# Decay attention with two feed-forward networks: warm-up products ahead of the first flip, the third block's loads between units 11 and 12, plain stores instead of an accumulating one, masks one place sooner

## The chip, the cores and the metric

The kernel runs on one core of a Trainium2 chip. Its engines are TensorE (PE), VectorE (DVE), ScalarE (ACT), GpSimd (POOL) and SyncE (SP), which only issues DMAs here; POOL can issue DMAs too. The metric is the device time of one execution in microseconds, the median of several runs. The granted clock is the share of TensorE's 2.4 GHz that it was given.

## The reference

```python
B, H, S, D = 4, 8, 768, 48                       # attention with a decaying state
for t in range(S):
    cur = einsum('bhd,bhe->bhde', u * k[t], v[t])
    y[t] = einsum('bhd,bhde->bhe', r[t], state + cur)
    state = w[:, :, None] * state + einsum('bhd,bhe->bhde', k[t], v[t])
x = y as (3072 tokens, 384)
x = (silu(x @ w_gate) * (x @ w_val)) @ w_out      # first network, 384 -> 1536 -> 384
h = x @ w_in                                      # second network, 384 -> 2048 -> 384
y = (h * tanh(softplus(h))) @ w_out2
```

## The kernel before

The 768 steps of the sequence are cut into six blocks j of 128; with the four batches b, a block is 512 columns. Each of the two networks multiplies in three products (L247 to L249): the operands are split into a high and a low part of a narrower type, and high by high, high by low and low by high are summed. A **unit** is one block j and one tile f of 128 hidden features of the first network: a gate (nine products into a buffer `mm`), a val (nine more) and, for the unit before, an out (nine into `acc` or `at`). ACT makes the sigmoid of the gate (L659, into a buffer `o`), DVE multiplies (L663), ACT makes the high part (L665, `g_hi`) and DVE the low part (L671, `g_lo`). There are two buffers `mm`, two each of `g_hi` and `g_lo`, and three of `o`.

Work beside the products is put between them by hand. Everything is issued in the order of the program; each engine runs its own instructions in that order, and no other.

- **The early loop** computes the attention of blocks 0 and 1, eight steps (j, b): masks (L479), own terms (L531), outputs (L498), `at_y` (L538), flips (transposes L592) and decays (L415) of the step after next. `warm(n)` puts n products of 128x512 on an idle buffer. Behind the loop the first two loads of block 2 (`rkv_sb`, `n_sb`) are issued.
- **The units** 0 to 13 alternate between block 0 and block 1 for f from 0 to 6; units 14 to 18 finish block 0, units 19 to 23 block 1, and then each block from 2 on has twelve units. The sum of block 1's first seven tiles stands in the `at` buffers (`besides`), is stored to `mid[1]` after unit 13, and the rest is added to it in DRAM by an accumulating DMA of POOL (L698) after unit 23.
- **A tick** decodes one tile of weights, which arrive as 64-bit numbers: ACT L156 and L199, DVE L164, L170, L205 (the tile before), L178 and L183, five DVE operations in a row; the second network's tiles have L205 on POOL and are stored and loaded again. `due` says how many ticks a unit has.
- **The strings `UNITS`** give the order within a unit: `rest` is the low part of the unit before, `mine` that of the unit itself, `fill` a place for steps of the attention of a later block, `tick` a place for a tick. `form` chooses the string. `KEYS`, `STATES`, `AHEAD`, `BEGIN`, `STEPS` and `SPREAD` list the steps that go into the places. In them `first` and `second` are L440 and L442 (POOL), `total` L448 (DVE), `sooner` and `later` L415 (POOL from block 2 on), `diag` two L453 (POOL), `keys` L462, `even` and `odd` the masks (L479) of the two halves of the heads.

The second network reads `mid[j]` back (`load_mid`, L853, three tiles `rows`), and `split_mid` (L861, L862 on DVE) splits them three units later.

Of the kernel before, what the change touches and what calls it, by code (L numbers as in the profile page):

```python
# [9 lines left out]
F32 = mybir.dt.float32  # L10
# [7 lines left out]
P = 128  # L18
CH = 128
NJ = S // CH  # L20
NB = B * CH
# [29 lines left out]
]  # L51
SPREAD = [
    "out state load2 diag1", "hi fade keys1", "low", "sum first2", "scores1 second2",
    "even1 total2", "odd1 later2 sooner2",
]

KEYS = [[(1, b, "keys")] for b in range(B)]
# [11 lines left out]
    "gate act val tick mul tick",  # L69
    "gate rest val act tick out mul tick",  # L70
    "gate tick rest val act fill tick out mul",
    "gate rest fill act val mul tick out fill tick fill tick",
    "gate rest fill act val fill mul mine tick tick out fill",
    "gate fill act val fill mul mine out fill",
    "gate fill act val mul tick mine fill out fill tick tick",
]

# [9 lines left out]
def tile_decay_attention_then_two_ffns(  # L87
# [28 lines left out]

    w2s = [dram.tile([P, 2, DM], F32, name=f"w2s{n}") for n in range(2 * NF2)]
    mid = [dram.tile([P, KC * NB], F32, name=f"mid{j}") for j in range(NJ)]
    ctx.enter_context(tc.manual_schedule())

    class Weights:
# [221 lines left out]
                start=True, stop=True,  # L343
            )

    warm(11)

    scores = [spool.tile([P, NPAIR, CH], F32, name=f"s{g}") for g in range(2)]
    for t in scores:
# [294 lines left out]
                at_part(j, b, part)  # L644


    gs, begun = {}, set()

    def ffn1_mm(j, f, which):
        hi, lo = xs[j, "x"]  # L650
# [23 lines left out]
    def ffn1_out(j, f, first, last):  # L674
        acc = accs
        if (j, f) in BESIDE:

            acc = besides
        if first:
            for m in range(KC):  # L680
                if acc is besides:
                    acc[m] = ps_at.tile([P, NB], F32, name="at")
                else:
                    acc[m] = ps_acc.tile([P, NB], F32, name=f"acc{m}")
        hi, lo = gs.pop((j, f))
        wt = weights.until((1, f, 2))
        for m in range(KC):
            product(acc[m], wt, cols(m), hi, lo, first, last)
        if last:
            for m in range(KC):  # L690
                o = opool.tile([P, NB], F32, name="o")
                if m == 1:
                    nc.vector.tensor_copy(o, acc[m])
                else:
                    nc.scalar.activation(o, acc[m], AF.Copy)
                rows = mid[j][:, m * NB : (m + 1) * NB]
                if j in begun:
                    nc.gpsimd.dma_start(out=rows, in_=o, accum_op=ALU.add)  # L698
                else:
                    nc.sync.dma_start(out=rows, in_=o)  # L700
            begun.add(j)

    class Filler:

# [37 lines left out]
    for n, now in enumerate(early):  # L742
# [14 lines left out]
        at_fade(*now)  # L757
        if now[0] == 0:
            at_state(*now)
        if n + 1 < len(early):  # L760
            at_flip(*now)
        if n >= B - 1:
            weights.tick()

        warm((2, 2, 2, 2, 3, 6, 6, 0)[n])

    for b in range(2):
        at_tiles(EARLY, b)
        load_at(EARLY, b)

# [12 lines left out]
    def unit1(n, fill=nothing, tick=nothing):  # L785

        j, f, _, _ = units[n]
        gate = val = act = None
        form = n if n < 2 else 2 if n < 2 * PAIRED else 3 if n < ready - 1 else 4 if n < ready else 5
        for part in UNITS[form if n < 24 else 6].split():  # L790
            if part == "gate":
                gate = ffn1_mm(j, f, 0)
# [30 lines left out]
    for n in range(len(units) - NF1):  # L823
        if n in beside:
            fill.flush()
            fill = Filler(*beside[n])
        due += 2 if n < 2 * PAIRED else 1.5 if n < ready else 0 if n < 24 else 1.3
        some = int(due) if weights.at < W_STORED + 2 else 0
        ticks = [weights.tick if i < some else nothing for i in range(3)]
        due -= int(due)  # L830
        turn = iter(ticks)
        unit1(n, fill, lambda: next(turn)())
# [16 lines left out]
    def load_mid(j):  # L849
        raw = []  # L850
        for c in range(KC):
            raw.append(mpool.tile([P, NB], F32, name="rows"))
            nc.sync.dma_start(out=raw[c], in_=mid[j][:, c * NB : (c + 1) * NB])  # L853
        xs[j, "m"] = (
            raw,
            *(xpools[j % 2].tile([P, KC, NB], F32R, name=f"x_{k}") for k in ("hi", "lo")),
# [211 lines left out]
```

## Time and profile before

| what | value |
|---|---|
| median of three runs | 970.05 us (968.21 to 971.46) |
| the profiled execution | 971.8 us |
| its span, first to last instruction | 969.8 us |
| PE busy | 949.0 us, 98% of the span |
| DVE, ACT, POOL busy | 635.5, 473.7 and 180.1 us |
| mean granted clock | 0.986 |

PE is the engine to look at: it is busy nearly all the time, so what counts is when it waited and at which clock it ran. In the timeline a row gives start and duration in us, the engine, the line, the operation with its operands and tiles, and in brackets how long the engine was idle ahead of it and which operation ended that idle time.

### The profile page before, as it was taken

What the parts mean: (1) busy time and instruction counts of PE and PEld (TensorE: products, weight loads), DVE (VectorE), ACT (ScalarE), POOL (GpSimd) and SP (SyncE); (2) the same over time, 40 slices, a digit from 0 to 9 for tenths busy, and PEclk for the clock granted to TensorE, in tenths of its full rate; (3) what the DMA queues carried; (4) which work ended last, traced back from release to release, by engine and by line L of the source; (5) the groups of instructions that cost most, each with busy time, mean ns of one, the idle gap of its engine ahead of it and who ended that gap; (6) DMA issues with size and microseconds to landing.
All of it is one profiled execution on the core that took longest, in us unless ns stands there. A gap on an engine that the chain in (4) does not pass through costs nothing.

```text
span 969.8 us, 14841 instructions
## 1 busy us (share of the span) xinstructions
PE 949.0 (98%) x5787; PEld 772.9 (80%) x5787; DVE 635.5 (66%) x1154; ACT 473.7 (49%) x841; POOL 180.1 (19%) x164
## 2 busy tenths in 40 slices
PE   8989998999799999999999999999999999999998
PEld 5868886778688878888888888888888888888886
DVE  7899878634567676832222338878778677787674
ACT  2345543323333433322122238777767676767674
POOL 4220003267565465523000000000000000000000
PEclk8899999999999999999999999999999999999999
DMA  8254433235665675321018640102001010000000
GB/s 324 105 195 147 131 98 109 74 113 152 187 207 190 195 223 185 116 98 50 1 38 270 194 149 1 33 1 66 0 33 33 1 42 25 0 33 1 33 1 32
DMA packets 35781, 94.21 MB, mean 97 GB/s; under 512 B 4224, under 2 KB 4352, under 8 KB 35712
## 3 DMA queue, kind: packets, MB, share of 16 engines
q1 hardware_dynamic: 35280, 92.49, 29.0%
q0 software_dynamic: 432, 0.79, 0.6%
q8 instruction: 45, 0.74, 0.3%
q14 instruction: 24, 0.20, 0.1%
HBM read 70.46 MB, written 22.81 MB: 96 GB/s over the span
## 4 chain that ended last, share of the span: by engine, by line
PE 72%; ACT 1%; DVE 1%; issue 0%
PE acc L247 10%; PE acc L248 10%; PE acc L249 10%; PE mm L247 9%; PE mm L248 9%; PE mm L249 9%; PE at L249 4%; PE at L248 4%; PE at L247 4%; PE at L521 2%; PE at L472 1%; PE at L552 0%; ACT e L908 0%; DVE g_lo L671 0%; DVE s L479 0%
## 5 line engine op out<-in xcount | busy, mean ns | idle before, releaser
L247 PE MATMUL mm<-x_hi,w_split 128*128 128x512 f32 x546 | 217.5, 398 | 5.9 <-DVE o L663 3.7
L248 PE MATMUL mm<-x_lo,w_split 128*128 128x512 f32 x546 | 214.3, 392 | 0.0
L249 PE MATMUL mm<-x_hi,w_split 128*128 128x512 f32 x546 | 213.7, 391 | 0.0
L248 PE MATMUL acc<-g_lo,w_split 128*128 128x512 f32 x483 | 188.7, 391 | 3.8 <-DVE g_lo L671 3.7
L247 PE MATMUL acc<-g_hi,w_split 128*128 128x512 f32 x483 | 189.6, 392 | 0.0
L249 PE MATMUL acc<-g_hi,w_split 128*128 128x512 f32 x483 | 188.3, 390 | 0.0
L663 DVE TENSOR_TENSOR o<-mm,o 128x512 f32<-128x512 f32 x72 | 49.8, 691 | 179.4 <-PE mm L249 143.1
L247 PEld LDWEIGHTS mm<-x_hi,w_split 128*128 128x128 f32 x546 | 103.3, 189 | 30.1 <-DVE o L663 4.2
L249 PEld LDWEIGHTS mm<-x_hi,w_split 128*128 128x128 f32 x546 | 103.4, 189 | 22.1
L248 PEld LDWEIGHTS mm<-x_lo,w_split 128*128 128x128 f32 x546 | 103.5, 190 | 20.7
L665 ACT ACTIVATE g_hi<-o 128x512 fp32r<-128x512 f32 x72 | 45.5, 632 | 137.4 <-DVE o L663 137.1
L248 PEld LDWEIGHTS acc<-g_lo,w_split 128*128 128x128 f32 x483 | 90.8, 188 | 23.5 <-DVE g_lo L671 4.5
L247 PEld LDWEIGHTS acc<-g_hi,w_split 128*128 128x128 f32 x483 | 90.6, 188 | 19.9 <-ACT g_hi L665 0.2
L249 PEld LDWEIGHTS acc<-g_hi,w_split 128*128 128x128 f32 x483 | 90.8, 188 | 18.9
L659 ACT ACTIVATE o<-mm 128x512 f32<-128x512 f32 x72 | 42.8, 594 | 111.0 <-PE mm L249 94.6
L895 ACT ACTIVATE e<-h 128x512 f32<-128x512 f32 x96 | 60.1, 626 | 53.0 <-DVE h L889 51.7
L902 ACT ACTIVATE e<-e 128x512 f32<-128x512 f32 x96 | 59.6, 621 | 49.7 <-DVE e L899 49.6
L909 DVE TENSOR_TENSOR h<-h,e 128x512 f32<-128x512 f32 x96 | 60.0, 688 | 20.5 <-ACT e L908 20.5
L671 DVE TENSOR_TENSOR g_lo<-o,g_hi 128x512 fp32r<-128x512 f32 x72 | 56.1, 780 | 22.4 <-ACT g_hi L665 22.3
L247 PE MATMUL at<-x_hi,w_split 128*128 128x512 f32 x174 | 67.7, 389 | 0.0
L248 PE MATMUL at<-x_lo,w_split 128*128 128x512 f32 x174 | 67.7, 389 | 0.0
L249 PE MATMUL at<-x_hi,w_split 128*128 128x512 f32 x174 | 67.7, 389 | 0.0
(105 smaller groups left out, 1349.5 us busy)
## 6 DMA issues: line engine op xcount, KB each, us to landing
w_raw<-w SPq DMA_DIRECT2D x68, 384.0 KB, 3.4
rkv_sb<-rkv_t SPq DMA_DIRECT2D x16, 768.0 KB, 4.9
w2s<-w_raw SPq DMA_DIRECT2D x32, 384.0 KB, 5.3
w_split<-w2s SPq DMA_DIRECT2D x32, 384.0 KB, 3.6
n_sb<-rk_n SPq DMA_DIRECT2D x16, 384.0 KB, 5.9
mid<-o SPq DMA_DIRECT2D x18, 256.0 KB, 2.3
rows<-mid SPq DMA_DIRECT2D x18, 256.0 KB, 2.6
y<-o SPq DMA_DIRECT2D x18, 256.0 KB, 2.3
```

The costliest lines, as they stand in the source:

```text
L247: nc.tensor.matmul(acc, lhsT=wt[:, 0, sl], rhs=hi, start=start, stop=False)
L248: nc.tensor.matmul(acc, lhsT=wt[:, 0, sl], rhs=lo, start=False, stop=False)
L249: nc.tensor.matmul(acc, lhsT=wt[:, 1, sl], rhs=hi, start=False, stop=stop)
L472: nc.tensor.matmul(ps[g][:, i, :], lhsT=a["k"][q, i, :], rhs=a["r"][q, i, :], start=True, stop=True,)
L521: nc.tensor.matmul(ps[q * QUAD : (q + 1) * QUAD, c, :], lhsT=lhsT, rhs=rhs, start=q not in begun_q, stop=ends[q] == n, skip_group_check=True,)
L659: nc.scalar.activation(sg, ps, AF.Silu)
L663: nc.vector.tensor_tensor(out=sg, in0=ps, in1=sg, op=ALU.mult)
L665: nc.scalar.activation(hi, sg, AF.Copy)
L671: eng.tensor_tensor(out=lo, in0=sg, in1=f32(hi), op=ALU.subtract)
L895: nc.scalar.activation(es[n], hs[n], AF.Exp)
L902: nc.scalar.activation(e, e, AF.Ln, bias=1.0)
L909: nc.vector.tensor_tensor(out=hs[n], in0=hs[n], in1=es[n], op=ALU.mult)
```

## The change

- `warm(11)` at the start becomes `warm(12)`, and in the first step of the early loop four more products stand ahead of the flip.
- The first two loads of block 2 leave their place behind the early loop. They are issued ahead of units 11 and 12.
- The strings of units 14 to 23 change: unit 14 makes the low part of unit 13 and its own, units 15 and on their own low part, ahead of the `out` of the unit before. `due` falls from 1.5 to 1 a unit in units 14 to 18.
- The accumulating DMA goes. Block 1's first sum is stored to a new DRAM tensor `begun`, its second to `mid[1]`, both by SP; `load_mid(1)` loads `mid[1]`, and POOL adds `begun` onto the loaded tiles with an accumulating DMA.
- In `SPREAD` both masks stand where `even` stood, and `total` one place later.

```diff
@@ SPREAD
-    "even1 total2", "odd1 later2 sooner2",
+    "mask1", "total2 later2 sooner2",
@@ UNITS
-    "gate rest fill act val mul tick out fill tick fill tick",
-    "gate rest fill act val fill mul mine tick tick out fill",
-    "gate fill act val fill mul mine out fill",
+    "gate rest fill act val mul tick mine out fill tick fill tick",
+    "gate fill act val mul tick mine out fill tick fill tick",
+    "gate fill act val fill mul mine tick tick out fill",
@@
+    begun = dram.tile([P, KC * NB], F32, name="begun")
@@
-    warm(11)
+    warm(12)
@@ ffn1_out
-                rows = mid[j][:, m * NB : (m + 1) * NB]
-                if j in begun:
-                    nc.gpsimd.dma_start(out=rows, in_=o, accum_op=ALU.add)
-                else:
-                    nc.sync.dma_start(out=rows, in_=o)
-            begun.add(j)
+                to = begun if acc is besides else mid[j]
+                nc.sync.dma_start(out=to[:, m * NB : (m + 1) * NB], in_=o)
@@ the early loop
+        if n == 0:
+            warm(4)
         if n + 1 < len(early):
             at_flip(*now)
@@
-    for b in range(2):
-        at_tiles(EARLY, b)
-        load_at(EARLY, b)
@@ unit1
-        form = n if n < 2 else 2 if n < 2 * PAIRED else 3 if n < ready - 1 else 4 if n < ready else 5
+        form = n if n < 2 else 2 if n < 2 * PAIRED else 3 if n == 2 * PAIRED else 4 if n < ready - 1 else 5
@@ the loop over units
+        if n in (2 * PAIRED - 3, 2 * PAIRED - 2):
+            ahead = order[EARLY * B + n - 2 * PAIRED + 3]
+            at_tiles(*ahead)
+            load_at(*ahead)
-        due += 2 if n < 2 * PAIRED else 1.5 if n < ready else 0 if n < 24 else 1.3
+        due += 2 if n < 2 * PAIRED else 1 if n < ready else 0 if n < 24 else 1.3
@@ load_mid
+            rows = slice(c * NB, (c + 1) * NB)
+            nc.sync.dma_start(out=raw[c], in_=mid[j][:, rows])
+            if j == 1:
+                nc.gpsimd.dma_start(out=raw[c], in_=begun[:, rows], accum_op=ALU.add)
```

Lines below the new ones carry numbers higher by one or two in the changed kernel. On SP, from the last load ahead of the early loop (`u_sb`) on, the rows before are these; `rkv_sb` and `n_sb` are block 2's loads, `w_raw` those of weights, `mid` the stores of the first network:

```order
L325 DMA u_sb<-u_n 128x384
L145 DMA w_raw<-w 128x768 x2
L303 DMA rkv_sb<-rkv_t 128x1536
L304 DMA n_sb<-rk_n 128x768
L303 DMA rkv_sb<-rkv_t 128x1536
L304 DMA n_sb<-rk_n 128x768
L145 DMA w_raw<-w 128x768 x28
L700 DMA mid_114<-o 128x512 x3
```

and now:

```order
L326 DMA u_sb<-u_n 128x384
L146 DMA w_raw<-w 128x768 x24
L304 DMA rkv_sb<-rkv_t 128x1536
L305 DMA n_sb<-rk_n 128x768
L146 DMA w_raw<-w 128x768 x2
L304 DMA rkv_sb<-rkv_t 128x1536
L305 DMA n_sb<-rk_n 128x768
L146 DMA w_raw<-w 128x768 x4
L698 DMA begun<-o 128x512 x3
```

The two pairs of loads moved behind 22 more loads of weights, each pair by itself. On DVE, from the end of unit 15's first tick to the multiply of unit 16, the rows before are (five `w_` rows are a tick, `state` is a sum of the attention's state):

```order
L183 SCALAR_TENSOR_TENSOR w_num<-w_raw,w_num 128x384
L568 TENSOR_TENSOR state<-at,state 48x4x48 x2
L164 TENSOR_SCALAR w_num<-w_num 128x384
L170 SCALAR_TENSOR_TENSOR w_num<-w_raw,w_num 128x384
L205 TENSOR_TENSOR w_split<-w_num,w_split 128x384
L178 TENSOR_SCALAR w_num<-w_num 128x384
L183 SCALAR_TENSOR_TENSOR w_num<-w_raw,w_num 128x384
L671 TENSOR_TENSOR g_lo<-o,g_hi 128x512
L568 TENSOR_TENSOR state<-at,state 48x4x48 x2
L663 TENSOR_TENSOR o<-mm,o 128x512
```

and now, from the multiply of unit 15 on, which the same first tick follows:

```order
L664 TENSOR_TENSOR o<-mm,o 128x512
L165 TENSOR_SCALAR w_num<-w_num 128x384
L171 SCALAR_TENSOR_TENSOR w_num<-w_raw,w_num 128x384
L206 TENSOR_TENSOR w_split<-w_num,w_split 128x384
L179 TENSOR_SCALAR w_num<-w_num 128x384
L184 SCALAR_TENSOR_TENSOR w_num<-w_raw,w_num 128x384
L672 TENSOR_TENSOR g_lo<-o,g_hi 128x512
L569 TENSOR_TENSOR state<-at,state 48x4x48 x4
L664 TENSOR_TENSOR o<-mm,o 128x512
```

The low part (`g_lo`) of unit 15 moved ahead of the sums, and the second tick is gone from between. On POOL, around the accumulating DMA after unit 23, the rows before are:

```order
L453 TENSOR_TENSOR s_230<-ident,bonus 128x512
L205 TENSOR_TENSOR w_raw<-w_num,w_raw 128x384
L462 TENSOR_TENSOR n_sb<-n_sb,tabn 128x384
L698 DMA mid_114<-o 128x512 x3
L440 TENSOR_TENSOR pr<-n_sb 128x384
```

and now:

```order
L454 TENSOR_TENSOR s_232<-ident,bonus 128x512
L206 TENSOR_TENSOR w_raw<-w_num,w_raw 128x384
L463 TENSOR_TENSOR n_sb<-n_sb,tabn 128x384
L441 TENSOR_TENSOR pr<-n_sb 128x384
```

The DMA is gone from there; POOL's last row of all is now the addition in `load_mid`.

## Rows read from the trace of the kernel before

**Rows 1.** Timeline of PE, the rows with the longest waits (in brackets).
```profile
14.63 0.55 PE L592 MATMUL at<-ident,y 128*128 128x128 f32 x3 [1.39 <-DVE y L538]
...
63.11 0.80 PE L247 MATMUL mm<-x_hi,w_split 128*128 128x512 f32 x1 [3.74 <-DVE o L663]
...
164.08 0.50 PE L248 MATMUL acc<-g_lo,w_split 128*128 128x512 f32 x1 [3.67 <-DVE g_lo L671]
...
246.45 0.50 PE L247 MATMUL mm<-x_hi,w_split 128*128 128x512 f32 x1 [2.21 <-ACT o L659]
...
258.43 0.65 PE L521 MATMUL at<-s,rkv_sb 128*32 128x128 f32 x16 [2.69 <-DVE s L479]
```

**Rows 2.** Stretches: length, busy time (instructions) by engine, granted clock, DMA share, GB/s.
```profile
15.00:31.00 16.00, 16.00 (x190) 12.80 (x190) 10.51 (x19) 2.77 (x7) 5.01 (x5) 0.51 0.94 359
160.00:180.00 20.00, 16.32 (x101) 12.29 (x100) 15.84 (x37) 7.24 (x14) 1.06 (x2) 0.91 0.21 60
240.00:260.00 20.00, 15.10 (x130) 11.43 (x129) 11.16 (x19) 6.16 (x14) 13.66 (x12) 0.91 0.62 156
```

**Rows 3.** Timeline of PE, the ninth product after the second wait.
```profile
66.55 0.40 PE L249 MATMUL mm<-x_hi,w_split 128*128 128x512 f32 x1
```

**Rows 4.** Timeline of DVE, one unit with two ticks, undisturbed.
```profile
128.25 0.69 DVE L663 TENSOR_TENSOR o<-mm,o 128x512 f32<-128x512 f32 x1 [0.94 <-PE mm L249]
...
130.80 0.69 DVE L671 TENSOR_TENSOR g_lo<-o,g_hi 128x512 fp32r<-128x512 f32 x1
...
134.37 0.69 DVE L663 TENSOR_TENSOR o<-mm,o 128x512 f32<-128x512 f32 x1 [0.94 <-PE mm L249]
```

**Rows 5.** Timeline of PE, outputs of three steps of the early loop.
```profile
15.85 1.95 PE L498 MATMUL at<-w_split,s 128*64 128x48 f32 x32
...
35.80 1.09 PE L498 MATMUL at<-w_split,s 128*64 128x48 f32 x32
...
40.17 1.19 PE L498 MATMUL at<-w_split,s 128*64 128x48 f32 x32
```

**Rows 6.** SP's timeline, then the page's DMA issues (KB each, us to landing).
```profile
10.97 0.33 SPq L301 DMA_DIRECT2D w_split<-kv_n  x1
...
w_split<-kv_n SPq DMA_DIRECT2D x8, 384.0 KB, 6.7
```

**Rows 7.** Timelines of DVE and (last row) POOL, around unit 0.
```profile
56.65 0.35 DVE L164 TENSOR_SCALAR w_num<-w_num 128x384 f32<-128x384 f32 x1
...
62.38 0.68 DVE L663 TENSOR_TENSOR o<-mm,o 128x512 f32<-128x512 f32 x1
...
71.94 0.69 DVE L671 TENSOR_TENSOR g_lo<-o,g_hi 128x512 fp32r<-128x512 f32 x1
...
59.13 2.91 POOL L415 TENSOR_TENSOR rkv_sb<-rkv_sb,tab 128x512 f32<-128x512 f32 x2
```

**Rows 8.** Timelines of POOL (first row) and DVE, units 15 and 16.
```profile
151.99 2.04 POOL L453 TENSOR_TENSOR s<-ident,bonus 128x512 f32<-128x512 f32 x2 [89.95 <-DVE bonus L448]
...
153.44 0.69 DVE L663 TENSOR_TENSOR o<-mm,o 128x512 f32<-128x512 f32 x1 [1.59 <-PE mm L249]
...
160.65 0.71 DVE L568 TENSOR_TENSOR state<-at,state 48x192 f32<-48x192 f32 x2
...
163.34 0.69 DVE L671 TENSOR_TENSOR g_lo<-o,g_hi 128x512 fp32r<-128x512 f32 x1
```

**Rows 9.** Timeline of ACT around unit 25, then the page's DMA issues.
```profile
245.80 0.60 ACT L659 ACTIVATE o<-mm 128x512 f32<-128x512 f32 x1 [5.77 <-DMA mid<-o]
...
mid<-o SPq DMA_DIRECT2D x18, 256.0 KB, 2.3
...
mid<-o POOLq DMA_DIRECT2D x3, 256.0 KB, 7.0
```

**Rows 10.** Timelines of SP and DVE, block 1's rows in the second network.
```profile
574.97 1.39 SPq L853 DMA_DIRECT2D rows<-mid  x3
...
605.02 0.42 DVE L861 CAST x_hi<-rows 128x512 fp32r<-128x512 f32 x1
```

More of the change, by code (lines that the diff above doesn't have):

```diff
@@ L644, in do @@
                 at_part(j, b, part)
-    gs, begun = {}, set()
+    gs = {}
     def ffn1_mm(j, f, which):
@@ L852, in load_mid @@
             raw.append(mpool.tile([P, NB], F32, name="rows"))
-            nc.sync.dma_start(out=raw[c], in_=mid[j][:, c * NB : (c + 1) * NB])
+            rows = slice(c * NB, (c + 1) * NB)
+            nc.sync.dma_start(out=raw[c], in_=mid[j][:, rows])
+            if j == 1:
+                nc.gpsimd.dma_start(out=raw[c], in_=begun[:, rows], accum_op=ALU.add)
         xs[j, "m"] = (
```

## The prediction

> **What bounds the kernel now.** I asked first for the stretches in which TensorE (PE) waited, since its products fill nearly the whole span: an edit is worth what it takes from these waits or from products run at the lower clock. The list of PE's waits, in order of time, has five that matter [rows 1]: 1.39 us ahead of the first flip (the transposes of L592), 3.74 us on a multiply of VectorE (DVE), 3.67 us on a low half (g_lo) of DVE, 2.21 us on ScalarE's (ACT's) sigmoid of a later unit, and 2.69 us on a mask. After 258 us the waits shown sum to a few tenths; from there to the end PE's own products are the time, and the change takes none away. So the whole case lies in the first 260 us.
>
> A wait costs more than itself. After the first, the granted clock was 0.51 of full from 15 to 31 us, that is 1.2 GHz, with PE busy all of the time [rows 2]. After the second, eight products took from 63.11 to 66.55, or 3.44 us [rows 3]; eight at 2.4 GHz take 8 x 6.12 / 27 = 1.81 (a unit of 27 products repeats each 134.37 - 128.25 = 6.12 us [rows 4]), so the slow spell cost 1.63. The stretches with the third and fourth wait show a mean of 0.91 [rows 2]; I put 1.63 on each of those spells too, as an estimate from the second. For the fifth I count none.
>
> **Part 1, four warm-up products ahead of the first flip (and one at the start).** PE has nothing in 13.24 to 14.63 but waits for y (L538). Four products of 128x512 at full clock are 0.9 us, so they fit into 1.39 and delay nothing. The twelfth at the start falls into a wait on DVE of half a microsecond. Cost nothing; if the cover were gone, 5 x 0.23 = 1.1 us. The gain hangs on the clock. In the slow stretch the three steps between the outputs (L498) at 15.85 and 35.80 took 19.95 us; the next step, at 2.4 GHz, took 40.17 - 35.80 = 4.37 [rows 5]. Three such steps are 13.1. DVE gives the same: busy 10.51 of 16 us [rows 2], which is 13.1 of 19.95, so it would then be the next limit. Gain 6.85. Bounds: 0 if the clock falls all the same; 8.0 if PE alone decides (16 us at half clock). I take 6.85, since a row at full clock shows it. Loads don't stop it: the second block's first ones are issued by 10.97 and land some 6.7 us later [rows 6], at 18, and the steps that use them come at 21 or later even when sped up.
>
> **Part 2, the third block's loads at units 11 and 12.** Before, these loads stand ahead of the units on SyncE (SP); GpSimd (POOL) has an empty queue and works on the data as they land. Its last two such multiplies start at 59.13, and the tick (the decoding of one weight) that DVE has running meanwhile takes from 56.65 to 62.38, 5.73 us [rows 7]. Undisturbed, a multiply and a tick together take 130.80 - 128.25 = 2.55 [rows 4], the tick 1.9 of it. So 3.8 us are lost to work that the two engines do at once; the multiply that PE waits for comes that much sooner, and its end at 59.3 meets PE's wish at 59.37. Gain 3.74 + 1.63. What is late next: DVE is full there. The second unit's low half started 71.94 - 62.38 = 9.56 after that multiply [rows 7]; moved up, it ends at 58.6 + 9.56 + 0.69 = 68.85, and PE, with 36 products of 0.227 from 59.37 and one more, asks at 67.76. Give back 1.1. Net 4.27.
> The same work of POOL now meets the ticks of units 12 and 13, some 6 us after the loads. There DVE idles 0.94 a unit, and the low half is ready 134.3 - 131.5 = 2.8 us ahead of PE [rows 4]. 3.8 us lost in one such unit makes it 1.0 late at worst, nothing where the collision falls across two units. I take 0.5, between the two. On SP the loads now stand behind 24 loads of weights, which wait for free buffers; POOL needs them only in unit 15, about 20 us later.
>
> **Part 3, the low half of a unit in the unit itself, fewer ticks.** In unit 15 POOL starts a chain (diagonal, keys, own products, decays) when DVE's bonus is done, at 151.99. DVE's multiply at 153.44 and its tick end at 160.65, 7.21 us where 2.55 is normal; sums and a second tick follow, and the low half starts at 163.34 [rows 8]. PE stood from 160.41 to 164.08. Changed, the chain starts at the same place, but the low half follows the first slow tick: 160.65 + 0.69 = 161.34. Left of the wait: 0.93. Gain 3.67 - 0.93 + 1.63 = 4.37. Ticks go from 1.5 to 1 a unit here, so the last weights of the first matrix are decoded just in time in unit 18. Exposed in full it costs one tick, 1.9; at two ticks a unit DVE still had 0.94 idle [rows 4], at one it has more, so I take 0.
>
> **Part 4, no accumulating DMA between units.** The fourth wait: ACT's sigmoid was held 5.77 us by the buffers of o, which the accumulating stores of POOL keep until they land, 7.0 us against 2.3 for those that SP issues [rows 9]. With SP's stores the buffer comes back 4.7 sooner, and the wait was 2.21. Gain 2.21 + 1.63 = 3.84. The sum moves to L855: POOL adds the stored part onto rows that were loaded. Those loads are issued at 574.97 and their first reader, a cast, runs at 605.02 [rows 10]: 30.0 us, less about 2.6 for the load and 7.0 for the addition, leaves 20. Cost nothing; POOL is idle there.
>
> **Part 5, both masks together.** The fifth wait, 2.69, is for the mask of the odd heads, which stood behind a multiply, a tick and a low half. It now follows the even one. The bonus takes its place one later; one operation changes sides, so DVE's work is the same. Gain 2.69.
>
> **Sum.** 6.85 + 4.27 - 0.5 + 4.37 + 3.84 + 2.69 = 21.5. The profiled execution took 971.8 (span 969.8), so 950.3 of that kind; it stood 1.75 above the median of 970.05, and I take the saving from the median: 948.5.
>
> **A rule that speaks against part 4.** The trace's only accumulating stores landed in 7.0 us, at a time when DVE did little [rows 9]; at 605 DVE is busy most of the time, and no row shows such a DMA under it. The Trainium skill, "SBUF — State Buffer", section "SBUF: two separate sides", says that a DMA issued from GpSimd needs descriptors which GpSimd cannot write while VectorE holds the port they share. The section "A bandwidth-pool intuition that's wrong" gives 620 ns alone against 3100 ns beside a copy, five times as long. By the row the sum stays at 948.5; by that ratio, as an estimate, it would be the late addition of rival 3, 956. No run here shows it yet.
>
> **Rivals.**
> 1. The clock falls in spite of the warm-ups. For: half a microsecond of waiting is left at the flip, the steps that follow are made of small products, and the clock did not come back for 16 us though PE was busy [rows 2]. Against: the same kind of steps from 35.8 on ran at 2.4 GHz with fewer warm-ups between [rows 5]. Part 1 gives nothing: 955.4. Half of it, 952.
> 2. Collisions of POOL and DVE move instead of going: the waits that I leave (1.1, 0.5 to 1.0, 0.93) each let the clock fall, 3 x 1.63 = 4.9, with a further 0.5: 953.9. For: each wait named with a clock in [rows 2] is followed by such a spell. Against: the three are each shorter than 1.39, the shortest wait that was.
> 3. Slower than before: the addition in the second network lands so late that DVE, in order, stands at the cast, and PE behind it. The place is L855 to the cast; it loses from 27.4 us of landing on, one for one, and the kernel is slower than before by 0.3% from 27.4 + 21.5 + 2.9 = 51.8 us, over seven times the 7.0 seen. Then 973 and more. Milder: at five times the row, 35 us, it loses 7.6: 956. Against both: POOL's stores took three times as long as SP's [rows 9], and the same factor once more, 21 us, is still hidden.
> 4. The change doesn't do what it says: PE's waits are put on operations that came last by the trace, and others may stand right behind them. With parts 1 to 3 worth nothing and only parts 4 and 5 real, 6.5 are left: 963.5. For no change all five would have to fail.
>
> **Chances.** Forecast (945 to 951.5): 0.62. Rival 1: 0.16. Rival 2: 0.11. The late addition at 956: 0.03. Rival 4 with 963: 0.03; no change: 0.03. Rival 3: 0.02. Within 0.3% is about what a measurement of this kernel can tell from no change. So faster 0.95, same 0.03, slower 0.02. The range: the low end has all that I gave back (1.1, 0.93, 0.5) returned and part 1 at 8.0: 948.5 - 2.5 - 1.2 = 944.8. The high end takes in rivals 1 and 2 and part of the exposed tick: 957.
>
> **What would show it.** Part 1: a granted clock near 1 from 15 to 31 us, the L498 groups 4 to 4.5 us apart. Part 2: POOL's first own products near 120 us instead of 57, no tick near 6 us ahead of the first multiply, and a wait near 1 us on the second low half. Part 3: a wait near 1 us in unit 16 instead of 3.67. Parts 4 and 5: no wait of PE on a sigmoid or on a mask. It would be wrong if a new wait over 2 us appears in units 11 to 18, if the slow stretch stays, or if DVE waits for rows behind 575 us.

## The result, and the profile after

The changed kernel took **947.96 us** (median of four runs, 947.70 to 948.35) against 969.67 (968.21 to 971.46) for the kernel before beside it: a ratio of 0.9776, with a 95% interval of 0.9758 to 0.9793. The prediction was 948.5, in a range of 944.8 to 957.0. The time came out as forecast; parts 1 and 5 of its sum did not, part 4 costs what the sum said only beside the old form of part 3, and that the total fits is in good part luck, as the experiments show. The changed kernel is also steadier: its runs lie within 0.7 us, while the medians of the kernel before, beside the other experiments, were 966.45, 970.46 and 968.82, and single runs of it lie between 964.19 and 973.89.

The profiled execution took 948.35 us. From the page of the changed kernel, its span, PE's and DVE's busy time, and the granted clock in 40 slices:

```profile
span 946.6 us, 14850 instructions
PE 938.5 (99%) x5792; PEld 764.4 (81%) x5792; DVE 634.5 (67%) x1154; ACT 473.3 (50%) x841; POOL 176.7 (19%) x164
PEclk9999999999999999999999999999999999999999
```

PE is busy 10.5 us less than before, with the same products to make and five more: that is time which it no longer spends at the lower clock (mean 1.000, before 0.986). The rest of the gain is waits. These are all the waits of PE over 0.4 us from 14 to 350 us (timeline of PE, changed kernel), to hold against the five of [rows 1]:

```profile
14.83 0.55 PE L593 MATMUL at<-ident,y 128*128 128x128 f32 x3 [0.42 <-DVE y L539]
...
61.51 0.51 PE L249 MATMUL at<-g_lo,w_split 128*128 128x512 f32 x1 [0.61 <-DVE g_lo L672]
...
150.08 0.50 PE L249 MATMUL acc<-g_lo,w_split 128*128 128x512 f32 x1 [0.96 <-DVE g_lo L672]
```

The first is the wait at the flip, cut from 1.39 by the four products. The second is what the prediction gave back in part 2 (1.1), the third what it left in part 3 (0.93). No sigmoid and no mask is waited for any more. The same row of a multiply of DVE (L663, now L664), taken from both traces, shows where the gain came in:

| row | before, us | after, us | ahead by | gained since the row above |
|---|---|---|---|---|
| first product of unit 0 | 52.59 | 45.20 | 7.39 | 7.39 (part 1) |
| multiply of unit 9 | 116.01 | 104.57 | 11.44 | 4.05 (part 2) |
| of unit 15 | 153.44 | 142.15 | 11.29 | -0.15 (collision moved) |
| of unit 17 | 173.28 | 157.80 | 15.48 | 4.19 (part 3) |
| of unit 25 | 246.43 | 226.87 | 19.56 | 4.08 (part 4) |
| of unit 27 | 263.97 | 241.48 | 22.49 | 2.93 (part 5) |

After that 0.7 more comes in until the end (969.8 - 946.6 = 23.2). Between these two executions every part gave what the sum said within 0.6 us. That is one pair of executions, though; the account at the end sets a second and a third execution beside it.

**The stretch from 15 to 31 us** (columns as in [rows 2]) and the outputs L499 in it, to hold against [rows 5]:

```profile
15.00:31.00 16.00, 16.00 (x340) 13.65 (x339) 15.95 (x29) 5.41 (x15) 7.42 (x7) 1.00 0.96 365
```
```profile
19.73 1.14 PE L499 MATMUL at<-w_split,s 128*64 128x48 f32 x32
...
23.73 1.14 PE L499 MATMUL at<-w_split,s 128*64 128x48 f32 x32
...
28.43 1.09 PE L499 MATMUL at<-w_split,s 128*64 128x48 f32 x32
```

The clock is 1.00 instead of 0.51, a step takes 4.0 to 4.7 us where it took 6.65 on the mean (19.95 us for three, [rows 5]), and DVE is now full (15.95 of 16 us): it is the next limit, as the prediction said.

**The collision that was moved.** DVE from the low half of unit 10 to the multiply of unit 11, then POOL's first products on the third block's data:

```profile
113.24 0.69 DVE L672 TENSOR_TENSOR g_lo<-o,g_hi 128x512 fp32r<-128x512 f32 x1
113.84 1.17 DVE L165 TENSOR_SCALAR w_num<-w_num 128x384 f32<-128x384 f32 x1
114.93 1.37 DVE L171 SCALAR_TENSOR_TENSOR w_num<-w_raw,w_num 128x384 uint32<-128x384 uint32 x1
116.23 1.64 DVE L206 TENSOR_TENSOR w_split<-w_num,w_split 128x384 fp32r<-128x384 f32 x1
117.79 1.44 DVE L179 TENSOR_SCALAR w_num<-w_num 128x384 uint32<-128x384 uint32 x1
119.16 0.55 DVE L184 SCALAR_TENSOR_TENSOR w_num<-w_raw,w_num 128x384 uint32<-128x384 uint32 x1
119.63 0.68 DVE L664 TENSOR_TENSOR o<-mm,o 128x512 f32<-128x512 f32 x1
```
```profile
113.52 1.28 POOL L441 TENSOR_TENSOR pr<-n_sb 128x384 f32<-128x384 f32 x1 [76.74 <-DMA n_sb<-rk_n]
114.87 1.02 POOL L443 TENSOR_TENSOR pr<-pr,u_sb 128x384 f32<-128x384 f32 x1
115.84 3.18 POOL L416 TENSOR_TENSOR rkv_sb<-rkv_sb,tab 128x512 f32<-128x512 f32 x2
```

A tick takes 5.79 us (113.84 to 119.63) as it did ahead of the first multiply in [rows 7]. Units are 6.12 us apart [rows 4] and the multiply before started at 110.69, so this one is 2.8 us late; PE asks for the low half 2.8 us after it is normally ready, and no wait appears. The prediction had put it one unit later. DVE makes the lag good in the next units.

**The addition in the second network.** From the timelines of POOL and SP, the DMA issues from 550 to 575 us, and DVE's first cast of block 1's rows:

```profile
555.68 2.80 POOL L855 DMA_DIRECT2D rows<-begun  x3 [118.94 <-DMA rows<-mid]
```
```profile
rows<-begun POOLq DMA_DIRECT2D x3, 256.0 KB, 5.3
```
```profile
582.11 0.42 DVE L863 CAST x_hi<-rows 128x512 fp32r<-128x512 f32 x1
```

It landed in 5.3 us, with DVE busy 5.96 of the 8 us from 555 to 563, and the cast runs some 20 us later without a wait. Rival 3 and its milder form did not happen. The factor of five that the Trainium skill gives ("SBUF — State Buffer", "A bandwidth-pool intuition that's wrong") does not show here, beside DVE operations of 0.42 to 0.69 us: the landing is shorter than the 7.0 of [rows 9].

### The profile page after: what moved, and what is told of

It reads as the page before. It is cut to its first block, busy times and chain, and to the rows that moved or that the text cites. A ratio compares the mean times of both kernels' runs of the same rounds, so it can differ in the third digit from the quotient of the medians.

```text
span 946.6 us, 14850 instructions
## 1 busy us (share of the span) xinstructions
PE 938.5 (99%) x5792; PEld 764.4 (81%) x5792; DVE 634.5 (67%) x1154; ACT 473.3 (50%) x841; POOL 176.7 (19%) x164
## 4 chain that ended last, share of the span: by engine, by line
PE 93%; DVE 3%; DMA 3%; ACT 1%; issue 0%; SPq 0%; DVEq 0%
PE mm L248 13%; PE mm L249 13%; PE mm L250 12%; PE acc L248 12%; PE acc L249 12%; PE acc L250 12%; PE at L249 5%; PE at L250 5%; PE at L248 5%; PE at L522 3%; DMA w_split<-rk_t 2%; PE at L473 2%; PE at L553 1%; DVE w_num L184 1%; DMA w_raw<-w 0%; DVE w_num L165 0%
## 5 line engine op out<-in xcount | busy, mean ns | idle before, releaser
L664 DVE TENSOR_TENSOR o<-mm,o 128x512 f32<-128x512 f32 x72 | 49.7, 690 | 164.1 <-PE mm L250 130.0
L672 DVE TENSOR_TENSOR g_lo<-o,g_hi 128x512 fp32r<-128x512 f32 x72 | 53.1, 738 | 21.6 <-ACT g_hi L666 21.6
```

Source lines behind the costliest of these rows:

```text
L664: nc.vector.tensor_tensor(out=sg, in0=ps, in1=sg, op=ALU.mult)
L672: eng.tensor_tensor(out=lo, in0=sg, in1=f32(hi), op=ALU.subtract)
```

## Experiments

All times are medians of four runs unless said otherwise; the changed kernel stands at 947.96. It was not run again beside the experiments, and kernels nearly the same as it took 948.36 to 948.71 there, so a difference below some 0.8 us shows nothing by itself. To undo a part means to put the changed kernel back to the old form in that part alone.

**Part 1: what are the four products ahead of the flip worth?** Five kernels bear on it. First, the changed kernel without them:

```diff
-        if n == 0:
-            warm(4)
```

> The changed kernel without the four warm-up products ahead of the first flip (the twelfth at the start stays). My theory: the wait of about 1.4 us ahead of the flip comes back, the granted clock falls to half from about 15 us on and stays there for some 16 us, and the steps between the L499 groups take about 7 us instead of 4.0; the time goes from 948.0 to about 955.4 (7.4 more). Rival: the steps got shorter for another reason (the loads of block 2 that are gone from the start, or the twelfth product); then the clock stays full and the time is 948 to 949.

Measured: 948.36 (947.86 to 948.92), against 955.4 expected: the rival's time. The clock does not need them in these four runs, and in the profiled one PE did not even wait at the flip (13.98 us). The next puts them behind the flip:

```diff
-        if n == 0:
-            warm(4)
...
-        warm((2, 2, 2, 2, 3, 6, 6, 0)[n])
+        warm((6, 2, 2, 2, 3, 6, 6, 0)[n])
```

> The changed kernel with the same four products moved from ahead of the first flip to behind it, so that the wait ahead of the flip is left open. Theory A, the open wait is what lets the clock fall: the stretch from 15 to 31 us is slow again and the time is about 955 to 956. Theory B, only the number of dense products around there counts: the clock stays full, the four products cost at most their 0.9 us, and the time is 948 to 949.

Measured: 948.42 (947.50 to 950.38); the profiled run is the one of 950.38, and it has the wait of 1.39 again. The next takes away the twelfth product at the start as well:

```diff
-    warm(12)
+    warm(11)
...
-        if n == 0:
-            warm(4)
```

> The changed kernel with none of the five added products (eleven at the start as before, none ahead of the flip). The run without the four alone was as fast as the changed kernel, and in its profile PE came to the flip later and did not wait. Theory A, the slow stretch of 16 us in the profile of before belonged to that execution and not to the kernel: this one, too, takes 948 to 949 in most executions, with single ones up to 7 us above. Theory B, the twelfth product at the start is what keeps the clock: the slow stretch is there in most executions and the median is 953 to 955.5.

Measured: 948.71, with single runs of 947.97, 948.06, 949.35 and 952.51. And the kernel before with the five products as its only change:

```diff
-    warm(11)
+    warm(12)
...
+        if n == 0:
+            warm(4)
```

> The kernel before with nothing but the warm-ups of the change (twelve at the start, four ahead of the first flip). My theory: part 1 stands by itself, 969.7 - 7.4 = about 962.3, with the four later waits of PE (3.7, 3.7, 2.2 and 2.7 us) all still there. Rival: DVE, which was nearly full from 34 us on, or the loads take part of it back; then it gains less than 5 and the time is above 964.5.

Measured: 967.79 (ten runs, 965.81 to 971.25) against 966.45 (thirteen runs) for the kernel before beside it; ratio 1.0002, interval 0.9978 to 1.0025. The 962.3 expected is missed by 5.5. So in the median part 1 is worth at most 0.75 us in the changed kernel and nothing that can be measured in the kernel before (by the interval, between 2.1 us gained and 2.4 lost), not 6.85. Last, the kernel before once more:

> The kernel before itself, profiled once more. Theory: the half clock from 15 to 31 us is in some executions and not in others, so a second profile will more likely than not have a granted clock above 0.9 there, PE's four later waits as they were (3.74, 3.67, 2.21, 2.69, each within half a microsecond), and a time of 964 to 969 if so. Rival: the slow stretch belongs to the kernel before, follows its wait of 1.39 us at the first flip each time, and shows 0.5 to 0.7 again with a time of 969 or more.

Measured: 968.20, one execution, and the stretch from 15 to 31 us ran at full clock. Of the four later waits two were within half a microsecond, as expected (3.33 and 3.68), and two were 0.65 us longer, the last one with a stretch at the lower clock behind it, which [rows 1] and the sum do not have:

```profile
240.57 0.54 PE L247 MATMUL mm<-x_hi,w_split 128*128 128x512 f32 x1 [2.85 <-ACT o L659]
...
253.15 0.64 PE L521 MATMUL at<-s,rkv_sb 128*32 128x128 f32 x16 [3.35 <-DVE s L479]
```
```profile
255.00:260.00 5.00, 5.00 (x17) 4.00 (x16) 0.00 (x0) 1.02 (x3) 1.89 (x2) 0.70 0.76 224
```

Here are the two kinds of execution, the first from the kernel without any added product (its run of 952.51), the second from this second profile of the kernel before: DVE's two pairs of L415 (L416), PE's flip, and the stretch.

```profile
8.95 1.54 DVE L416 TENSOR_TENSOR w_split<-w_split,tab 128x512 f32<-128x512 f32 x2
11.06 2.83 DVE L416 TENSOR_TENSOR w_split<-w_split,tab 128x512 f32<-128x512 f32 x2 [0.56 <-DMA w_split<-rk_t]
```
```profile
14.41 0.55 PE L593 MATMUL at<-ident,y 128*128 128x128 f32 x3 [1.39 <-DVE y L539]
```
```profile
15.00:31.00 16.00, 16.00 (x253) 13.21 (x251) 11.85 (x22) 2.77 (x7) 5.58 (x6) 0.69 0.95 362
```

and

```profile
8.90 3.84 DVE L415 TENSOR_TENSOR w_split<-w_split,tab 128x512 f32<-128x512 f32 x4
```
```profile
13.26 0.55 PE L592 MATMUL at<-ident,y 128*128 128x128 f32 x3
```
```profile
15.00:31.00 16.00, 15.31 (x320) 13.02 (x316) 15.91 (x28) 5.06 (x15) 6.88 (x6) 1.00 0.92 350
```

The wait at the flip is not a property of the order. It stands where a load (`w_split` from `rk_t`) lands a few tenths too late for DVE, which then makes the second pair beside POOL; where the load is there in time, the four operations run in one go and PE never waits. Of the five profiles without the four products three have the wait (the first of before, that of 952.51, and the one with the products behind the flip), and two have not. Of the three, the first two went into a long stretch at the lower clock (mean 0.51 and 0.69), and the one with six products behind the flip had the lower clock for some 3 us only (0.90). In the changed kernel's own profile the load was late too (DVE waited 0.62 us for it), the four products filled the wait, and the clock stayed. All fourteen profiles of this document go the same way. In eight DVE waited 0.26 to 0.74 us for this load: the three without the four products waited 1.39 us at the flip and show a clock of 0.50 to 0.53 from 15 to 18 us; the five with them waited 0.42 or 0.43 us and show 1.00 there. In the other six the load was late by 0.16 us or not at all, and PE did not wait at the flip. So part 1 takes away a loss that some executions have: 4.2 us in the run of 952.51, which is that far behind the changed kernel at the first product of unit 0 and at the end, and 7.4 in the first profile of before. How many executions of the kernel before have it is open: two were profiled, and one had it.

That part 1 leaves the other four waits alone is seen in PE's timeline of the kernel before with the products alone:

```profile
55.27 0.78 PE L247 MATMUL mm<-x_hi,w_split 128*128 128x512 f32 x1 [3.37 <-DVE o L663]
...
156.34 0.50 PE L248 MATMUL acc<-g_lo,w_split 128*128 128x512 f32 x1 [3.66 <-DVE g_lo L671]
...
238.71 0.50 PE L247 MATMUL mm<-x_hi,w_split 128*128 128x512 f32 x1 [2.17 <-ACT o L659]
...
250.69 1.08 PE L521 MATMUL at<-s,rkv_sb 128*32 128x128 f32 x16 [2.74 <-DVE s L479]
```

**Part 2: are the loads' place and POOL's products the cause of the 3.74?** The changed kernel with the loads back behind the early loop:

```diff
+    for b in range(2):
+        at_tiles(EARLY, b)
+        load_at(EARLY, b)
...
-        if n in (2 * PAIRED - 3, 2 * PAIRED - 2):
-            ahead = order[EARLY * B + n - 2 * PAIRED + 3]
-            at_tiles(*ahead)
-            load_at(*ahead)
```

> The changed kernel with the first two loads of block 2 back behind the early loop. My theory: POOL's first own product for block 2 runs at about 49 us instead of 113, a tick of DVE beside it takes about 5.7 us instead of 1.95, PE waits about 3.7 us for the multiply of unit 0, a slow spell follows, and the time is about 4.0 above 948.0, 952.0; the slow tick at 114 us is gone, which gives nothing back since no wait stood behind it. Rival: the slow operations come from the loads' traffic and not from POOL; then DVE's operations are slow from about 43 us on, when the loads run, and not from the start of POOL's product on.

Measured: 952.52 (951.70 to 953.44), 4.56 more. DVE's operations while the loads ran, and after POOL had begun on the data; then POOL; then PE:

```profile
47.43 0.55 DVE L184 SCALAR_TENSOR_TENSOR w_num<-w_raw,w_num 128x384 uint32<-128x384 uint32 x1
...
49.43 1.06 DVE L165 TENSOR_SCALAR w_num<-w_num 128x384 f32<-128x384 f32 x1
50.41 1.38 DVE L171 SCALAR_TENSOR_TENSOR w_num<-w_raw,w_num 128x384 uint32<-128x384 uint32 x1
51.71 1.62 DVE L206 TENSOR_TENSOR w_split<-w_num,w_split 128x384 fp32r<-128x384 f32 x1
53.25 1.41 DVE L179 TENSOR_SCALAR w_num<-w_num 128x384 uint32<-128x384 uint32 x1
```
```profile
49.25 1.02 POOL L441 TENSOR_TENSOR pr<-n_sb 128x384 f32<-128x384 f32 x1 [12.30 <-DMA n_sb<-rk_n]
50.35 1.02 POOL L443 TENSOR_TENSOR pr<-pr,u_sb 128x384 f32<-128x384 f32 x1
51.33 3.12 POOL L416 TENSOR_TENSOR rkv_sb<-rkv_sb,tab 128x512 f32<-128x512 f32 x2
```
```profile
55.79 0.80 PE L248 MATMUL mm<-x_hi,w_split 128*128 128x512 f32 x1 [3.61 <-DVE o L664]
```

DVE's operations have their normal length at 47.43, while the loads are on the way (issued from 43.38 us on, landing 6.3 to 6.7 us later), and two and a half to four times that from POOL's start on. It is POOL's work on the data, not the transfers.

**Part 3: the low half and the ticks.** The changed kernel with the old strings of units 14 to 23, the old choice of `form`, and 1.5 ticks:

```diff
-    "gate rest fill act val mul tick mine out fill tick fill tick",
-    "gate fill act val mul tick mine out fill tick fill tick",
-    "gate fill act val fill mul mine tick tick out fill",
+    "gate rest fill act val mul tick out fill tick fill tick",
+    "gate rest fill act val fill mul mine tick tick out fill",
+    "gate fill act val fill mul mine out fill",
...
-        due += 2 if n < 2 * PAIRED else 1 if n < ready else 0 if n < 24 else 1.3
+        due += 2 if n < 2 * PAIRED else 1.5 if n < ready else 0 if n < 24 else 1.3
```

> The changed kernel with the strings of units 14 to 23 and the rate of ticks (1.5) of before. My theory: in unit 16 PE waits 3.7 us for the low half instead of 0.96, and a slow spell of about 1.6 follows in most executions: 4.2 more than 948.2, about 952.4, or 950.9 where the clock does not fall. Rival: with the load moved, POOL's chain of unit 15 meets DVE at another place and the old strings cost less than 1.5.

Measured: 952.25 (952.12 to 953.50), 4.29 more, with one new wait of PE:

```profile
152.61 0.80 PE L249 MATMUL acc<-g_lo,w_split 128*128 128x512 f32 x1 [3.66 <-DVE g_lo L672]
```

It is the 3.67 of [rows 1] to a hundredth, and behind it the granted clock was 0.57 from 152 to 156 us. With the old strings the wait at unit 25 did not come back.

**Part 4: the accumulating store.** The changed kernel with block 1's sum added in DRAM by POOL again, and no addition in the second network:

```diff
-                to = begun if acc is besides else mid[j]
-                nc.sync.dma_start(out=to[:, m * NB : (m + 1) * NB], in_=o)
+                rows = mid[j][:, m * NB : (m + 1) * NB]
+                if j in begun:
+                    nc.gpsimd.dma_start(out=rows, in_=o, accum_op=ALU.add)
+                else:
+                    nc.sync.dma_start(out=rows, in_=o)
+            begun.add(j)
...
-            if j == 1:
-                nc.gpsimd.dma_start(out=raw[c], in_=begun[:, rows], accum_op=ALU.add)
```

> The changed kernel with the accumulating store of POOL back behind unit 23 and no addition in the second network. My theory: ACT's sigmoid of unit 25 waits over 5 us for a buffer of o, PE waits 2.2 us and a slow spell of 1.6 us follows: 3.8 to 4.1 more than 948.2, 952.1. Rival: the buffer is not what is late; then the wait is gone with the other changes and the time stays at 948.

Measured: 949.10 (948.81 to 949.96), only 1.14 more, where the prediction had 3.84; the two profiled executions are 0.46 apart. So the store is dear only beside something else that the change also took away. The same edit together with that of part 3:

> The changed kernel with parts 3 and 4 both undone: the accumulating store of block 1 by POOL, and the old strings of units 14 to 23 with 1.5 ticks a unit. Alone, the old strings cost 4.05 us (952.25 against 948.2) and the accumulating store 0.9 (949.1). Theory: the store is dear only beside the old order, in which the second network's weights are written and read earlier and the buffers of o are given back later; then ACT's sigmoid of unit 25 is held again for over 5 us, PE waits 2 us or more there, and the time is the two prices as the prediction had them, 948.2 + 4.05 + 3.84 = 956.1. Rival: the store's price is 0.9 whatever stands ahead of it, PE's wait there is below 1 us, and the time is 948.2 + 4.05 + 0.9 = 953.2.

Measured: 956.89 (955.53 to 959.67), 8.93 more, where the two alone sum to 5.43. The profiled execution is the fastest, 955.53, which is 3.29 above that with the old strings alone (952.24); what the slower ones add to it, no profile shows. ACT's sigmoid of unit 25, POOL's stores ahead of it and PE behind it, first with the store alone:

```profile
228.34 0.60 ACT L659 ACTIVATE o<-mm 128x512 f32<-128x512 f32 x1 [3.92 <-DMA mid<-o]
```
```profile
224.25 2.82 POOL L698 DMA_DIRECT2D mid<-o  x3 [4.22 <-ACT o L695]
```
```profile
228.99 0.50 PE L247 MATMUL mm<-x_hi,w_split 128*128 128x512 f32 x1 [0.36 <-ACT o L659]
```

and with the old strings and ticks too, with the next load of SP:

```profile
234.73 0.60 ACT L659 ACTIVATE o<-mm 128x512 f32<-128x512 f32 x1 [5.95 <-DMA mid<-o]
```
```profile
228.62 2.81 POOL L698 DMA_DIRECT2D mid<-o  x3 [4.22 <-ACT o L695]
```
```profile
235.38 0.50 PE L247 MATMUL mm<-x_hi,w_split 128*128 128x512 f32 x1 [2.76 <-ACT o L659]
```
```profile
229.42 0.33 SPq L145 DMA_DIRECT2D w_raw<-w  x1
```

With the old ticks the buffer came back 6.1 us after POOL began to issue, with the new ones 4.1 us. With the old ones SP issues a load of 384 KB of weights 0.8 us after POOL's stores (before: 1.0 us after); with the new ones that load comes 5.3 us after they began, when the first buffer is already back. In the four profiles in which a load follows within 1.0 us (both of before, that with part 1 alone, and the one with parts 3 and 4 undone) the stores landed in 6.7 to 7.1 us, in the one in which none does, in 5.5. The rows fit a store that shares the transfer with a load; no run here moves the load alone, so that part stays argued.

**Part 5: the masks.**

```diff
-    "mask1", "total2 later2 sooner2",
+    "even1 total2", "odd1 later2 sooner2",
```

> The changed kernel with the two masks in two places again, and the bonus one place sooner. My theory: PE waits about 2.7 us for the odd mask in unit 26 and 0.3 us in a later unit, mostly without a slow spell: 2.9 more than 948.2, 951.1, up to 952.7 with a spell. Rival: the mask was late only because the sigmoid of the unit before had been late (the accumulating store pushed the units together), and with that gone it costs under 0.5.

Measured: 954.51 (953.91 to 955.11), 6.55 more, over twice the 2.69. PE's timeline has a wait at a mask, but twelve units later than in the kernel before, and a stretch at the lower clock behind it:

```profile
328.74 1.08 PE L522 MATMUL at<-s,rkv_sb 128*32 128x128 f32 x16 [3.54 <-DVE s L480]
```
```profile
330.00:340.00 10.00, 10.00 (x49) 8.13 (x46) 3.14 (x6) 3.39 (x9) 3.93 (x4) 0.78 0.78 253
```

The tick ahead of that mask, on DVE, and what POOL did meanwhile:

```profile
322.87 1.44 DVE L165 TENSOR_SCALAR w_num<-w_num 128x384 f32<-128x384 f32 x1
...
322.80 2.65 POOL L416 TENSOR_TENSOR rkv_sb<-rkv_sb,tab 128x512 f32<-128x512 f32 x2
```

At unit 26, where the kernel before lost 2.69, it loses 0.29, as little as the rival said of that place. A mean of 0.78 over 10 us is 4.4 us at half the clock, some 2.2 lost; with the 3.54 that is 5.7 of the 6.55. In both places that waited, unit 26 of the kernel before and unit 38 here, the late mask stood behind a tick that ran beside POOL's decays. Why unit 26 hardly waits here is not shown.

**Two versions beyond the change.** DVE's first operation of a tick, L164, took 1.3 us where it met POOL's L422 in the early loop (L165 and L423 in the changed kernel, 1.30 and 1.27 us in two steps). In the first version the tick stands ahead of POOL's decays in the last steps, and the warm-up products of these steps ahead of the flip:

```diff
+        if n >= B - 1:
+            weights.tick()
         at_early(n + 2, prepare)
...
         if n == 0:
             warm(4)
+        elif n >= 4:
+            warm((3, 6, 6, 0)[n - 4])
         if n + 1 < len(early):
             at_flip(*now)
-        if n >= B - 1:
-            weights.tick()
-        warm((2, 2, 2, 2, 3, 6, 6, 0)[n])
+        if n < 4:
+            warm((2, 2, 2, 2)[n])
```

> The changed kernel with one more move: in the last four steps of the early loop the decoding tick stands ahead of POOL's decays instead of behind them, and the warm-up products of those steps ahead of the flips. Theory: DVE's first operation of such a tick took 1.3 us beside POOL's decay (L422) and 0.35 alone, so the steps that PE spends behind DVE there are shorter by up to 1 us each in two of them: 948.2 - 1.9 = 946.3 at best. Rival: the early loop is set by the chain of one step to the next and not by DVE's ticks; then nothing is gained, 948.2, or up to 1 us is lost where the flips now stand behind more products, 949.2.

Measured: 946.78 (946.05 to 947.65), 1.2 less than the changed kernel, of at most 1.9 expected; in its profile that operation takes 0.35 us in each of these steps, and the multiply of unit 0 starts at 49.19 instead of 51.20. What the moved warm-up products do in this was not tried alone. The second has besides the second of block 2's two pairs of loads at unit 16:

```diff
-        if n in (2 * PAIRED - 3, 2 * PAIRED - 2):
-            ahead = order[EARLY * B + n - 2 * PAIRED + 3]
+        if n in (2 * PAIRED - 3, 2 * PAIRED + 2):
+            ahead = order[EARLY * B + (n > 2 * PAIRED)]
```

> The kernel with the tick ahead of the decays, and besides the second pair of block 2's loads not at unit 12 but at unit 16, so that POOL's chain of products beside DVE in units 12 to 15 is cut in two. Theory: the wait of 0.96 us that the changed kernel has left at 150 us, on a low half made while POOL multiplies, goes, and it stands 0.5 to 0.96 us below the kernel with the tick move alone. Rival: POOL's products of the second pair meet another unit's tick further on, the same wait appears there, and the time is the same within 0.3 us or longer by as much.

Measured: **945.04** (944.98 to 945.39), ratio to the kernel before 0.9759 (0.9722 to 0.9796), and the steadiest of all. The 0.96 at 150 us is gone from PE's waits. Two rows of POOL, the first from the version with the tick move alone, show why:

```profile
141.64 1.12 POOL L441 TENSOR_TENSOR pr<-n_sb 128x384 f32<-128x384 f32 x1
```
```profile
144.35 1.01 POOL L441 TENSOR_TENSOR pr<-n_sb 128x384 f32<-128x384 f32 x1 [2.48 <-DMA n_sb<-rk_n]
```

POOL's products now wait 2.48 us for their load, and DVE has the tick behind the multiply of unit 15 to itself for that long: the next multiply starts at 147.14 instead of 149.42, and at the one after (154.70 against 155.77) 1.07 us is left as gain. The two profiled executions are 1.05 apart (946.05 and 945.00). The 1.74 between the two medians is more than that, and more than the 0.96 expected; the version with the tick move alone has runs up to 947.65, and no profile shows what they add.

## Why the prediction was right, and where it was not

**The waits and their causes** were right but for part 1; of part 4's cause a piece stays argued. Parts 2 to 5, undone alone, each brought back a wait of the named kind, those of parts 2 and 3 at the named place with the named size (3.61 for 3.74, 3.66 for 3.67), that of part 4 at the named place but small (0.36 for 2.21), and that of part 5 twelve units later. Part 1's wait came back in some executions only. What was left of the waits (0.61, 0.96) and the moved collision (0.15 for 0.5) came within half a microsecond of what was given back for them.

What each part gave can be read between the same rows as in the table above, from three profiles of the old order: that of before, the second of before, and that of the kernel before with part 1 alone.

| us gained in | sum | before | before, second | with part 1 alone |
|---|---|---|---|---|
| part 1 | 6.85 | 7.39 | -1.28 | -0.11 |
| part 2 | 4.27 | 4.05 | 4.95 | 3.82 |
| collision moved | -0.5 | -0.15 | -0.15 | -0.15 |
| part 3 | 4.37 | 4.19 | 5.44 | 4.23 |
| part 4 | 3.84 | 4.08 | 4.72 | 4.03 |
| part 5 | 2.69 | 2.93 | 5.13 | 5.66 |
| the whole span | 21.5 | 23.2 | 19.5 | 18.1 |

Another 0.6 to 0.7 us comes in behind these rows. In the third profile part 1 stands on both sides. In the second it is negative: the old order did not wait at the flip there, and the changed kernel makes five products more (1.1 us by the price in the prediction).

**Part 2** was sized at 4.27 and cost 4.56 to undo; **part 3** at 4.37, and 4.29 to undo. The exposed tick of unit 18, priced at 0, did not show. Part 3's estimate of 1.63 for the slow spell is borne out: the wait itself explains only 3.66 - 0.96 = 2.7 of the 4.29, and a clock of 0.57 over 4 us is 3.4 us at half the clock, some 1.7 lost.

**Part 1 was mis-sized: 6.85 against at most 0.75 in the median.** The step that failed is the last one of the sum: it took the long stretch of one execution from a median of several. The prediction saw that the profiled execution stood only 1.75 above the median, and did not ask whether the stretch of 0.51 was in the other executions. The second profile of before shows it was not in that one. Against the first profile the term is right (7.39). The prediction also took the wait of 1.39 for a property of the order, an operation of DVE that comes late; the runs showed that it stands only where a load for DVE lands some tenths late, and the trace that it was written from had DVE waiting 0.26 us for that load at 10.97.

**Part 5 was mis-sized the other way: 2.69 against 6.55** undone, and 2.93, 5.13 and 5.66 in the table. The step that failed is "for the fifth I count none": no slow spell was counted behind this wait, since the one execution that had been read showed none there. Two of the three profiles of the old order have one behind the same wait, and so has the changed kernel with part 5 undone, where the wait came twelve units later and was longer (3.54).

**Part 4 was sized at 3.84**; it gave 4.03 to 4.72 in the table, and is 1.14 undone alone, 956.89 - 952.25 = 4.64 beside the old ticks. Parts 3 and 4 together are 8.93, against 8.21 in the sum. The prediction named the landing of 7.0 us as a price of POOL's stores; the runs showed that it depends on what is on the way beside them.

**The sum.** Undone from the changed kernel, the parts cost 0.75 + 4.56 + 8.93 + 6.55 = 20.8, which from 947.96 is 968.75, among the medians of before (966.45 to 970.46). The predicted 21.5 met the measured 21.7 in good part by luck: the excess in part 1 (6.1) was nearly made up by the other parts: 4.56 against 3.77 for part 2 with its collision, 0.7 more in parts 3 and 4, 3.9 more in part 5. That the undone parts sum so well is no proof that each has a price of its own, since parts 3, 4 and 5 cost other amounts beside other neighbours. Two errors of one kind, a spell counted in part 1 that the medians do not bear out and one left out of part 5 that two of three profiles have, took each other's place. Rival 1 did not happen: the clock of the changed kernel stayed at 1.00. That part 1 gives the median next to nothing is what rival 1 had, but for another reason, and without its 955.4. Rival 2 did not: no wait was left above 0.96 us, and no slow spell followed one. Of rivals 3 and 4 nothing showed.

## What to carry to other kernels

One profile of a kernel that is close to a wait shows one of its executions: before a stretch at the lower clock is put into a sum that starts from the median, or left out of it, profile the kernel twice, or compare the clock of the profiled run with those of the others. A wait is worth removing even when the median gains little by it, if some executions pay several microseconds for it. And where an elementwise engine feeds PE, time the other one's bulk work by when its loads are issued: issuing a load later was enough here to keep POOL out of DVE's way.

## What was not expected of the hardware

- DVE beside POOL: a tick of five operations took 5.79 us beside POOL's four products, against 1.9 alone [rows 4]. Four of the five grew by 0.8 to 1.1 us each, and a product of POOL took 1.0 to 1.6. The Trainium skill, "SBUF — State Buffer", "SBUF: two separate sides", says that the two engines share a pair of ports which one instruction holds to its end; the rows agree in that each operation that grew did so by near the length of one product.
- The clock after a wait of the same length differs from execution to execution. Behind the wait on the sigmoid of unit 25, 2.76 us in the kernel with the old strings and store, the granted clock from 235 to 245 us was 1.00; behind 2.85 us in the second profile of before it was 0.83.
- Some tenths decide over microseconds: where a load came 0.56 us after DVE was ready for it, PE waited 1.39 us and then ran on at a clock of 0.54 from 15 to 26 us, and the run took 952.51; where it came in time, a kernel with one warm-up product more took 948.08. Two unprofiled runs of the first kernel took 947.97 and 948.06.
